# Loads, transposes and a batch's first stage moved within the prologue of an FFT and FFN kernel

## The chip, the cores and the metric

The kernel runs on one core of a Trainium2 chip. Its time is the device time of that core in microseconds (us), the median of several executions. A core has five engines that each work through their own list of instructions in order: PE (TensorE, matrix products), DVE (VectorE), ACT (ScalarE), POOL (GpSimd) and SP (SyncE). DMA transfers are issued from the lists of SP, ACT and POOL, and an issue that must wait for something holds up everything behind it in its list.

## What is computed

```python
def _attn_ref(x, filt_r, filt_i):
    X = np.fft.rfft(x, axis=1)
    F = (filt_r + 1j * filt_i)[None, :, :]
    Y = X * F
    y = np.fft.irfft(Y, n=x.shape[1], axis=1)
    return y.astype(np.float32)

def _moe_ref(x, w_in, w_out):
    h = np.maximum(x @ w_in, 0.0)
    return (h * h @ w_out).astype(np.float32)
```

x has 8 batches of 3008 rows and 256 columns in float32. Each batch goes through a real FFT along its rows, is multiplied by a filter (1505 frequencies by 256 columns, a real and an imaginary part), and comes back through the inverse FFT. The 24064 rows then go through a feed-forward network: w_in (256 x 2048), the square of the positive part, w_out (2048 x 256).

## The kernel before

**The FFT of a batch** is done as matrix products with constant tables, since 3008 = 64 x 47. It has four stages. *Stage A* (`unit_a`, 16 units for each batch from 1 on): one product over the 47, PSUM tile psA, copied to the tile u by ACT (even units) or DVE (odd units, batches 1 and 2); four units fill one tile u, which SP writes to a buffer dU in device memory (`write_u`). `read_u` brings it back in another order as ut. *Stage B* (`unit_b`, 12 units): products of ut with the table sSB (psB); DVE multiplies by the filter sF into prod, and for batches from 1 on two DMAs on POOL add the two halves of prod. *Stage P* (`unit_p`): products with the table sSP (psP), copied to ze, written to dZ; `read_z` brings dZ back as zt, in four parts c. *Stage Y* (`unit_y`, 16 units): products of zt (psY), copied to yt, the input of the network.

**Batch 0 is done ahead of everything else**, in a prologue, by other means. x is loaded in six halves (`load_wide` on SP, 512 KB each, in the order of `HALVES`), cast by DVE (`cast_wide`), and `chunk_a0` does stage A so that its output uT lies transposed; four passes, two classes of rows each. `turn_u` turns uT back with eight products with a unit matrix (psT), six calls in all, each copied to ut by two engines that it is given. Then a loop over k does two `unit_b` (whose output is first copied by ACT into ub), one `turn_u` and one `unit_p0`. Banks of PSUM come in turn from three tags (psH, psF, psO, two buffers each) through `bank_pair`. `turn_f` (DVE) puts the second half of the filter in place, once for each quarter of it (`FC`).

**Loads on POOL** go in this order before the change: a one-element copy into `tiny` that waits for the second half-load of x and so holds the rest back; 18 loads of the filter in four quarters; both halves of w_in (`load_win`, two loads each); the first two of eight loads of batch 1's x (`load_x`). When the products of the prologue are issued, `load_rest` follows: a second copy into `tiny`, which waits for zt, then the other x loads and w_out (`load_wout`). SP carries the loads of x, the tables (`load_const`), dZ, zt, dU, ut and all stores of the result.

**The trip of z.** Between the last `unit_p0` and the first `unit_y` dZ is written and read back. PE does 22 products of zeros there (`fill`, 128 x 512), which nothing uses.

**The main loop** has 8 turns s for each of 47 groups of 512 rows. Turn s does `ffn_g1` (psH: four products of 512 columns, with ACT's positive part into h), part of the second product of the group before (`ffn_g2` for the first and last group, `products` with `sums` for the rest, a scheme with seven products in place of eight), and DVE's square (`ffn_sq`). w_in's first half is read in turns 0 to 3 of a group, its second half in turns 4 to 7; w_out from turn 8 on. The FFT work of batches 1 to 7, and the end of batch 0's, is laid between by `fft_plan`: each unit has a due time in turns; `fixed` units have their half-turn, `units` look for a free one near theirs, and `moves` (loads, reads, `settle_f`, `settle_sp`) are added to theirs. For batch 1 the list has all 16 `unit_a` at turns 3 to 11.5, `read_u` at 12.5, `unit_b` from 16.5 to 30, and the first `unit_y` at 38. By the rule of `fft_plan` the last `unit_p` of batch 1 falls on turn 34, after the change on 33.5; the last `unit_a` of batch 2 on 44.5, after the change on 42. `settle_f` and `settle_sp` bring the filter and sSP from the form that batch 0 uses to that of the others.

Of the kernel before, what the change touches and what calls it, by code (L numbers as in the profile page):

```python
# [104 lines left out]
def kernel(  # L105
# [9 lines left out]
    nc = tc.nc  # L115
# [64 lines left out]
    def load_x(b, k):  # L180

        c, i = divmod(k, 2)
        if i == 0:
            x16s[(b, c)] = p_x16.tile([96, 8, D], F16, tag="x16", name=f"x16_{b}_{c}")
        t = x16s[(b, c)][:, 4 * i:4 * i + 4, :]
        m = slice(8 * c + 4 * i, 8 * c + 4 * i + 4)
        if b + 1 < B:
            v = xrows[b * S:b * S + 96 * NM, :].rearrange("(p m) d -> p m d", m=NM)
            nc.gpsimd.dma_start(out=t, in_=v[:, m, :])
        else:  # L190
            v = xrows[b * S:b * S + S, :].rearrange("(p m) d -> p m d", m=NM)
            nc.gpsimd.dma_start(out=t[0:80], in_=v[0:80, m, :])
            nc.gpsimd.dma_start(out=t[80:94], in_=v[80:94, m, :])
# [11 lines left out]
    xw16, xw32 = {}, {}  # L205
# [60 lines left out]
    def load_win(i):  # L266
        c = slice(1024 * i, 1024 * i + 1024)
        for k in range(2):
            nc.gpsimd.dma_start(out=sWin[:, k, c], in_=moe_w_in[128 * k:128 * k + 128, c])

    def load_wout(i):
        c = slice(8 * i, 8 * i + 8)
        nc.gpsimd.dma_start(out=sWout[:, c, :],
                            in_=moe_w_out.rearrange("(jt r) c -> r jt c", r=128)[:, c, :])
# [7 lines left out]
    for k in range(2):  # L282
        c = slice(12 * k, 12 * k + 12)
# [1 line left out]
        load_const(sSP[:, c, :], dPA, k)  # L285
        load_const(sSPx[k], dPB, k)
    tiny = const.tile([1, 2], F16, name="tiny")
    nc.gpsimd.tensor_copy(out=tiny[:, 0:1], in_=xw32[1][0:1, 0, 0:1])
    for c in FC:
        load_f(*c)  # L290
    for k in range(2):
        load_win(k)
    for k in range(2):
        load_x(1, k)

    def load_rest():

        nc.gpsimd.tensor_copy(out=tiny[:, 1:2], in_=ztiles[0][0:1, 0, 0:1])
        for k in range(2, 6):
            load_x(1, k)  # L300
        for k in range(2):
            load_wout(k)
        for k in range(6, 8):
            load_x(1, k)

    def fill(n):

        ps = psO("fill").rearrange("p a d -> p (a d)")
        for _ in range(n):
            nc.tensor.matmul(ps, zero[:, 0:128], zero, start=True, stop=True)  # L310
# [25 lines left out]
    def chunk_a0(k, *cs):  # L336

        for c in cs:
            banks, groups = bank_pair(f"psA_0_{c}_{k}")
            for dt in range(2):  # L340
                for i in range(4):
                    m = 4 * k + i
                    o = banks[dt][:, 96 * i:96 * i + 96]
                    d = slice(128 * dt, 128 * dt + 128)
                    nc.tensor.matmul(o, xw16[2 * (c % 2)][:, m, d], s0[:, c // 2, :],
                                     start=True, stop=False)
                    nc.tensor.matmul(o, xw16[1][0:120, m, d], s0[0:120, 2 + c, :],
                                     start=False, stop=True)
            for dt in range(2):
                m = 32 * c + 16 * k  # L350
                o = uT[:, dt, :, m:m + 16].rearrange("p c (m q) -> p m c q", q=4)
                pv = banks[dt][:, 0:384].rearrange("p (m c q) -> p m c q", m=4, q=4)
                if (pair_engine() is nc.scalar) if len(groups) == 1 else (dt == 0):
                    nc.scalar.copy(out=o, in_=pv)
                else:
                    nc.vector.tensor_copy(out=o, in_=pv)

    def turn_u(k, *engs):

        banks, groups = bank_pair(f"psT_{k}")  # L360
        for i in range(4):
            for dt in range(2):
                o = banks[i // 2][:, (i % 2) * D + 128 * dt:(i % 2) * D + 128 * dt + 128]
                nc.tensor.matmul(o, uT[:, dt, 4 * k + i, :], ident, start=True, stop=True)
        for i in range(2):
            eng = engs[i % len(engs)]
            o = uts[0][:, 4 * k + 2 * i:4 * k + 2 * i + 2, :]
            pv = banks[i].rearrange("p (a d) -> p a d", d=D)
            if eng is nc.scalar:
                eng.copy(out=o, in_=pv)  # L370
            else:
                eng.tensor_copy(out=o, in_=pv)
# [271 lines left out]
    def fft_plan():  # L644

        fixed, units, moves = [], [], []
        for b in range(1, B):
            f = (b * S // TG) * SLOTS - (48 if b > 1 else 40)
            d = 0
            if b == 1:  # L650
                for n in range(4, 16):
                    fixed.append(((n if n < 8 else n + 2 if n < 12 else 2 * n - 7) + n % 2 / 2,
                                  unit_y, 0, n))
                moves.append((7.5, read_z, 0, 3))
                for a in range(16):
                    fixed.append(((3 if a < 8 else 4) + a / 2, unit_a, b, a))
                for q in range(8):
                    moves.append((1 + q, settle_f, 3 * q, 3 * q + 3))
                moves.append((4, settle_sp))
                moves.append((12.5, read_u, b))  # L660
                d = 7
            else:
                for a in range(16):
                    if a % 2 == 0 and b > 2:
                        moves.append((f + ((-57 + 2.3 * a) if b == 3 else (-66 + 2.75 * a)),
                                      load_x, b, a // 2))
                    units.append((f + (-16 + a, -46 + 2.1 * a, -56 + 2.75 * a)[min(b, 4) - 2],
                                  unit_a, b, a))
                moves.append((f + (5.5 if b == 2 else -6.5), read_u, b))
            for p in range(12):  # L670
                r = 16.5 + 13.5 * p / 11 if b == 1 else 9 + 25 * p / 11 if b == 2 else -2 + 36 * p / 11
                units.append((f + r, unit_b, b, p))
                if b == 1 and 2 <= p < 10:
                    moves.append((f + r, load_x, 2, p - 2))
                units.append((f + r + (4 if b == 1 else 7 - 2.5 * p / 11), unit_p, b, p))
            for c in range(4):
                moves.append((f + (40 + d / 14 * 3, 43, 48, 54)[c] - d, read_z, b, c))
            for n in range(16):
                (fixed if n < 4 else units).append((f + YN[n] - d, unit_y, b, n))
        work, used, done = {}, set(), {}  # L680
        for r, *u in fixed:
            h = int(2 * r)
            used.add(h)
            work.setdefault(h, []).append(u)
        rank = (unit_b, unit_p, unit_y, unit_a)
        for r, *u in sorted(units, key=lambda u: (rank.index(u[1]), u[0])):
            after = done.get((u[0], u[1]), -1)
            h = min((h for h in range(max(int(2 * r) - 3, after + 1), int(2 * r) + 12)
                     if h not in used),
                    key=lambda h: (sum(h + i in used for i in (-2, -1, 1, 2)) > 2) * 2  # L690
                    + abs(h - int(2 * r)))
            used.add(h)
            done[(u[0], u[1])] = h
            work.setdefault(h, []).append(u)
        for r, *u in moves:
            work.setdefault(int(2 * r), []).append(u)
        return work
# [7 lines left out]
    for n, cs in enumerate(((0, 2), (0, 2), (1, 3), (1, 3))):  # L705
        for h in HALVES[n + 2:n + 3] if n > 1 else HALVES[2 * n:2 * n + 2]:
            cast_wide(*h)
        chunk_a0(n % 2, *cs)
    uts[0] = p_ut.tile([128, NC, D], F16, tag="ut", name="ut_0")
    turn_u(0, nc.scalar, nc.vector)  # L710
    turn_u(1, nc.scalar, nc.scalar)
    turn_u(2, nc.scalar, nc.vector)
    for k in range(8):
        if k < 6:
            for p in (2 * k, 2 * k + 1):
                for c in FC:
                    if c[0] == 2 * p:
                        turn_f(*c)
                if k > 1 and p % 2:
                    unit_p0(k - 2)  # L720
                unit_b(0, p)
        if 0 < k < 4:
            turn_u(k + 2, nc.scalar, nc.vector)
        if k > 5:
            unit_p0(k - 2)
    read_z(0, 0)
    read_z(0, 1)
    load_rest()
    fill(22)
    for n in range(4):  # L730
        unit_y(0, n)
    prologue[0] = False
# [5 lines left out]
    for s in range((NG + 1) * SLOTS):  # L738
        g, k = divmod(s, SLOTS)
# [46 lines left out]
```

## Time and profile before

| what | value |
|---|---|
| median of 7 runs | 775.01 us (772.49 to 779.17) |
| the profiled execution, its time | 774.29 us |
| its span from first to last instruction | 772.2 us |
| PE busy | 744.5 us (96%) |
| DVE busy | 646.9 us (84%) |
| ACT busy | 571.9 us (74%) |
| POOL busy | 188.5 us (24%) |
| mean granted clock of TensorE | 0.989 |
| first psH of the main loop | 51.14 us |

In the profile's lists a line gives its start and its length in us, the engine, the line of the kernel, the operation, the tile written and the tiles read, and how many instructions were merged; in brackets stands the idle time of the engine ahead of it and what ended that. "POOL ... DMA_DIRECT2D" is the issue of a transfer, not the transfer. The busy time of PE is modelled from the pipelined products, so a product's length includes its drain.

### The profile page before, as it was taken

What the parts mean: (1) busy time and instruction counts of PE and PEld (TensorE: products, weight loads), DVE (VectorE), ACT (ScalarE), POOL (GpSimd) and SP (SyncE); (2) the same over time, 40 slices, a digit from 0 to 9 for tenths busy, and PEclk for the clock granted to TensorE, in tenths of its full rate; (3) what the DMA queues carried; (4) which work ended last, traced back from release to release, by engine and by line L of the source; (5) the groups of instructions that cost most, each with busy time, mean ns of one, the idle gap of its engine ahead of it and who ended that gap; (6) DMA issues with size and microseconds to landing.
All of it is one profiled execution on the core that took longest, in us unless ns stands there. A gap on an engine that the chain in (4) does not pass through costs nothing.

```text
span 772.2 us, 19474 instructions
## 1 busy us (share of the span) xinstructions
PE 744.5 (96%) x8148; PEld 547.2 (71%) x8148; DVE 646.9 (84%) x734; ACT 571.9 (74%) x843; POOL 188.5 (24%) x262
## 2 busy tenths in 40 slices
PE   6777999999999999999999999999999999999998
PEld 3644666777778777777778777787777777777776
DVE  4748898799979898898889889798989999878873
ACT  2646777778877887778877887778887777777773
POOL 4320382033403232223212323133311232000000
PEclk8799999999999999999999999999999999999999
DMA  9987699477677546764677455855447433321011
GB/s 301 184 179 151 153 178 224 123 186 145 130 199 150 114 103 150 211 135 90 121 188 171 104 127 110 205 135 123 99 97 214 97 76 96 97 70 55 29 57 56
DMA packets 107184, 104.87 MB, mean 136 GB/s; under 512 B 9960, under 2 KB 94504, under 8 KB 106200
## 3 DMA queue, kind: packets, MB, share of 16 engines
q1 hardware_dynamic: 82408, 77.80, 33.6%
q0 software_dynamic: 24544, 25.64, 24.2%
q8 instruction: 64, 1.05, 0.5%
q10 hardware_dynamic: 144, 0.18, 0.1%
q14 instruction: 24, 0.20, 0.1%
HBM read 58.95 MB, written 48.23 MB: 139 GB/s over the span
## 4 chain that ended last, share of the span: by engine, by line
PE 84%; DVE 8%; DMA 3%; issue 2%; ACT 2%; SPq 1%; POOL 0%; ACTq 0%; DVEq 0%
PE psH L505 37%; PE psX L618 19%; PE psY L618 14%; PE psY L475 3%; PE psA L326 2%; PE psB L387 2%; PE psP L439 2%; DVE h L516 2%; DVE prod L400 2%; PE psO L525 2%; DMA prod<-prod 1%; DMA dZ<-ze 1%; DMA zt<-dZ 1%; PE fill L310 1%; DVE sum L591 1%
## 5 line engine op out<-in xcount | busy, mean ns | idle before, releaser
L509 ACT ACTIVATE h<-psH 128x1024 f16<-128x1024 f32 x376 | 384.9, 1024 | 154.8 <-PE psH L505 152.7
L505 PE MATMUL psH<-yt,sWin 128*128 128x512 f16 (+7 forms) x1728 | 387.5, 352 | 1.4 <-DVE yt L484 1.0
L516 DVE TENSOR_TENSOR h<-h 128x2048 f16<-128x2048 f16 (+1 forms) x192 | 229.8, 1197 | 47.4 <-ACT h L509 47.1
L407 POOL DMA_DIRECT2D prod<-prod x168 | 139.7, 970 | 432.5 <-DVE prod L400 390.1
L505 PEld LDWEIGHTS <-sWin 128*128 128x128 f16 x1728 | 152.3, 98 | 101.5 <-issue 6.1
L618 PEld LDWEIGHTS <-sum 128*128 128x128 f16 x2880 | 177.6, 98 | 20.0
L618 PEld LDWEIGHTS <-h 128*128 128x128 f16 x2160 | 133.7, 98 | 20.9
L400 DVE TENSOR_TENSOR prod<-psB,sF 128x1024 f16<-128x1024 f32 x84 | 102.3, 1219 | 13.6 <-PE psB L387 13.5
L618 PE MATMUL psX<-sT,sum 128*128 128x128 f16 x1440 | 102.4, 219 | 0.0
L618 PE MATMUL psY<-sT,sum 128*128 128x128 f16 x720 | 69.6, 219 | 0.0
L330 ACT CAST u<-psA 96x512 f16<-96x512 f32 x96 | 55.6, 580 | 2.7 <-PE psA L326 2.3
L594 DVE TENSOR_TENSOR sum<-sum,h 128x2048 f16<-128x2048 f16 x45 | 55.0, 1222 | 1.0
L618 PE MATMUL psY<-sWout,h 128*128 128x128 f16 x720 | 55.0, 219 | 0.0
L618 PE MATMUL psX<-sT,h 128*128 128x128 f16 x720 | 54.9, 219 | 0.0
L618 PE MATMUL psY<-sWout,sum 128*128 128x128 f16 x720 | 54.7, 219 | 0.0
L597 DVE TENSOR_TENSOR sum<-h 128x2048 f16<-128x2048 f16 x45 | 54.8, 1217 | 0.0
L600 DVE TENSOR_TENSOR sum<-h,sum 128x2048 f16<-128x2048 f16 x45 | 54.7, 1216 | 0.0
L591 DVE TENSOR_TENSOR sum<-h 128x2048 f16<-128x2048 f16 x45 | 54.7, 1216 | 0.0
L484 DVE CAST yt<-psY 128x376 f16<-128x376 f32 x62 | 33.7, 544 | 24.8 <-PE psY L475 24.8
L475 PEld LDWEIGHTS <-zt 112*128 112x128 f16 x512 | 34.1, 99 | 22.2 <-issue 8.4
L441 ACT CAST ze<-psP 128x512 f16<-128x512 f32 x84 | 49.0, 583 | 0.4 <-PE psP L439 0.2
L475 PE MATMUL psY<-sC,zt 112*128 112x94 f16 x512 | 43.2, 207 | 6.0 <-DMA zt<-dZ 3.6
(70 smaller groups left out, 612.9 us busy)
## 6 DMA issues: line engine op xcount, KB each, us to landing
zt<-dZ SPq DMA_DIRECT2D x64, 192.0 KB
dU<-u SPq DMA_DIRECT2D x28, 384.0 KB
prod<-prod POOLq DMA_DIRECT2D x168, 64.0 KB, 2.8
dZ<-ze SPq DMA_DIRECT2D x28, 384.0 KB
x<-in_x_dram POOLq DMA_DIRECT2D x48, 192.0 KB, 5.2
ut<-dU SPq DMA_DIRECT2D x7, 1024.0 KB
out_dram<-top SPq DMA_DIRECT2D x31, 128.0 KB
out_dram<-bot SPq DMA_DIRECT2D x31, 128.0 KB
```

The lines of the kernel that those rows point to most:

```text
L330: nc.scalar.copy(out=o, in_=pv)
L400: nc.vector.tensor_mul(out=prod, in0=pv.unsqueeze(1).to_broadcast([128, 2, 2, D]), in1=sF[:, :, 2 * p:2 * p + 2, :])
L407: nc.gpsimd.dma_start(out=prod[64 * i:64 * i + 64, 0], in_=prod[64 - 64 * i:128 - 64 * i, 1], accum_op=mybir.AluOpType.add)
L475: nc.tensor.matmul(ps[:, 94 * jj:94 * jj + 94], zt[:, 4 * (g % 2) + jj, dt * 128:(dt + 1) * 128], sSY, start=True, stop=True)
L505: nc.tensor.matmul(ps[:, i, o:o + n], sWin[:, dt, jt * 128:(jt + 1) * 128], yts[b][:, dt, r:r + n], start=(dt == 0), stop=(dt == 1))
L509: nc.scalar.activation(out=h2[:, 2 * s:2 * s + 2, :], in_=ps, func=AF.Relu)
L516: nc.vector.tensor_mul(out=v, in0=v, in1=v)
L591: nc.vector.tensor_add(out=t, in0=a21, in1=a22)
L594: nc.vector.tensor_sub(out=t, in0=f[5], in1=a11)
L597: nc.vector.tensor_sub(out=t, in0=a11, in1=a21)
L600: nc.vector.tensor_sub(out=t, in0=a12, in1=f[6])
L618: nc.tensor.matmul(o[:, t, :], f[p][:, q, 128 * t:128 * t + 128], sg["w"][p][:, q, :], start=(m == 0 and p in (1, 2)), stop=(q == 7), skip ...
```

## The change

The first copy into `tiny` reads the fourth half-load of x instead of the second, so the loads of the filter wait for that. Behind the filter, POOL loads x of batch 1 (parts 0 and 1, then 2 to 5, which stand after `chunk_a0` in the program) and only then the first half of w_in. The second half of w_in, x parts 6 and 7 and w_out follow behind the second copy into `tiny`. Four and two products of zeros are added after the first two passes of `chunk_a0`. Two `turn_u` instead of three are done ahead of the loop, and the third one in its first trip; the second one is copied by ACT and DVE instead of ACT alone. In the trip of z twelve `unit_a` of batch 1 take the place of 16 of the 22 fills. `fft_plan` keeps the four others at turns 8 to 9.5 and has new due times for batches 1 and 2.

```diff
-    nc.gpsimd.tensor_copy(out=tiny[:, 0:1], in_=xw32[1][0:1, 0, 0:1])
+    nc.gpsimd.tensor_copy(out=tiny[:, 0:1], in_=xw32[1][0:1, 4, 0:1])
     for c in FC:
         load_f(*c)
     for k in range(2):
-        load_win(k)
-    for k in range(2):
         load_x(1, k)
 
     def load_rest():
 
         nc.gpsimd.tensor_copy(out=tiny[:, 1:2], in_=ztiles[0][0:1, 0, 0:1])
-        for k in range(2, 6):
+        load_win(1)
+        for k in range(6, 8):
             load_x(1, k)
         for k in range(2):
             load_wout(k)
-        for k in range(6, 8):
-            load_x(1, k)
...
                 moves.append((7.5, read_z, 0, 3))
-                for a in range(16):
-                    fixed.append(((3 if a < 8 else 4) + a / 2, unit_a, b, a))
                 for q in range(8):
                     moves.append((1 + q, settle_f, 3 * q, 3 * q + 3))
-                moves.append((4, settle_sp))
-                moves.append((12.5, read_u, b))
+                moves.append((10, settle_sp))
+                for a in range(12, 16):
+                    fixed.append((2 + a / 2, unit_a, b, a))
+                moves.append((10.5, read_u, b))
...
-                moves.append((f + (5.5 if b == 2 else -6.5), read_u, b))
+                moves.append((f + (2 if b == 2 else -6.5), read_u, b))
             for p in range(12):
-                r = 16.5 + 13.5 * p / 11 if b == 1 else 9 + 25 * p / 11 if b == 2 else -2 + 36 * p / 11
+                r = 14 + 15 * p / 11 if b == 1 else 6 + 28 * p / 11 if b == 2 else -2 + 36 * p / 11
                 units.append((f + r, unit_b, b, p))
                 if b == 1 and 2 <= p < 10:
                     moves.append((f + r, load_x, 2, p - 2))
-                units.append((f + r + (4 if b == 1 else 7 - 2.5 * p / 11), unit_p, b, p))
+                units.append((f + r + (4.5 if b == 1 else 7 - 2.5 * p / 11), unit_p, b, p))
             for c in range(4):
-                moves.append((f + (40 + d / 14 * 3, 43, 48, 54)[c] - d, read_z, b, c))
+                moves.append((f + (40 + d / 14, 43, 48, 54)[c] - d, read_z, b, c))
...
         chunk_a0(n % 2, *cs)
+        if n < 2:
+            fill(4 - 2 * n)
     uts[0] = p_ut.tile([128, NC, D], F16, tag="ut", name="ut_0")
+    for k in range(2, 6):
+        load_x(1, k)
+    load_win(0)
     turn_u(0, nc.scalar, nc.vector)
-    turn_u(1, nc.scalar, nc.scalar)
-    turn_u(2, nc.scalar, nc.vector)
+    turn_u(1, nc.scalar, nc.vector)
...
-        if 0 < k < 4:
+        if k < 4:
             turn_u(k + 2, nc.scalar, nc.vector)
...
     load_rest()
-    fill(22)
+    for a in range(12):
+        unit_a(1, a)
+    fill(6)
     for n in range(4):
         unit_y(0, n)
```

## The prediction

> **What bounds the kernel now.** I read the slices of the page first, then the busy times of four stretches (columns: start:end, length, then busy time and count of PE, weight loads, DVE, ACT, POOL, then granted clock, DMA share, GB/s).
>
> ```profile
> PE   6777999999999999999999999999999999999998
> PEclk8799999999999999999999999999999999999999
> ...
> 0.00:51.10 51.10, 36.26 (x308) 25.86 (x309) 27.13 (x46) 21.29 (x37) 18.20 (x36) 0.85 0.90 223
> 51.10:84.90 33.80, 29.11 (x183) 16.55 (x182) 25.10 (x41) 22.36 (x30) 1.38 (x3) 0.98 0.80 168
> 84.90:140.00 55.10, 51.28 (x545) 36.59 (x544) 50.67 (x55) 40.82 (x63) 26.34 (x36) 1.00 0.85 182
> 140.00:772.20 632.20, 627.84 (x7119) 468.18 (x7116) 544.03 (x594) 487.44 (x714) 142.57 (x188) 1.00 0.52 123
> ```
>
> From 140 us on PE idles 4.4 us of 632: nothing to gain there, and whatever the start gives reaches the end whole. What can move is the prologue up to the first psH at 51.14 us, the turns s = 0 to 15 (PE idle 33.80 - 29.11 = 4.7 us) and batch 1 (55.10 - 51.28 = 3.8 us idle). Next the clock in single microseconds, and the order of time of DVE, PE and POOL in the prologue.
>
> ```profile
> 14.00:15.00 1.00, 0.00 (x0) 0.00 (x0) 1.00 (x2) 0.00 (x0) 0.07 (x1) 0.91 1.11 314
> 15.00:16.00 1.00, 0.95 (x13) 0.95 (x14) 0.00 (x0) 0.00 (x0) 0.00 (x0) 0.50 1.09 306
> ...
> 25.00:26.00 1.00, 0.37 (x6) 0.20 (x3) 0.77 (x2) 1.00 (x3) 1.00 (x3) 0.97 0.95 138
> ...
> 49.00:50.00 1.00, 0.95 (x12) 0.98 (x13) 0.00 (x0) 0.44 (x1) 1.00 (x3) 0.50 0.90 141
> ```
>
> ```profile
> 25.41 0.69 DVE L372 CAST ut<-psT 128x512 f16<-128x512 f32 x1 [0.23 <-PE psT L364]
> 26.13 1.25 DVE L248 COPY sF<-sF 64x1536 f16<-64x1536 f16 x2
> ...
> 26.25 1.03 PE L387 MATMUL psB<-ut,sSB 128*128 128x256 f16 x8 [0.88 <-DVE ut L372]
> 41.78 4.91 PE L310 MATMUL fill<-zero 128*128 128x512 f16 x22
> 49.05 0.47 PE L475 MATMUL psY<-sC,zt 112*128 112x94 f16 x4 [2.25 <-DMA zt<-dZ]
> ...
> 7.07 0.70 POOL L288 CAST tiny<-xw 1x1 f16<-1x1 f32 x1 [6.63 <-DMA xw<-in_x_dram]
> 22.91 0.57 POOL L241 DMA_DIRECT2D sF<-in_filt_r_dram  x1 [2.31 <-DMA sF<-in_filt_r_dram]
> 24.22 0.57 POOL L241 DMA_DIRECT2D sF<-in_filt_i_dram  x1
> 24.78 2.17 POOL L269 DMA_DIRECT2D sWin<-in_moe_w_in_dram  x4
> 47.10 0.18 POOL L298 COPY tiny<-zt 1x1 f16<-1x1 f16 x1 [19.09 <-DMA zt<-dZ]
> ```
>
> The clock is at 0.50 from 14.8 to 25.9 us, and again from 49.0 to 52.3. The first product (psB) waits for the copy of the third turn_u, not of the first. PE is through with unit_p0 at 41.78, fills, and waits for zt until 49.05.
>
> **1. The gate on POOL.** The four `load_const` issues on SP at 7.03, 8.49, 9.78 and 11.06 wait for halves 2 to 5 of x, so the fourth landed near 9.8. The gate moves by some 2.6 us, and 18 filter issues, the x loads and win(0) behind it move with it. Does anyone wait? A POOL issue here waits for the one eight before it (the tensors named fit). So FC0 had landed by 19, FC1 by 24.2 (the issue at 24.22 no longer waits), and FC3, last issued at 24.2, by 32 with the median 7.4 us of the filter loads. DVE turned them at 26.13, 29.41 and 38.15: slack of 5 to 7 us. Take off 2.6 here and some 3.6 for an earlier DVE (below) and between +1 and -1 us is left: hidden, but barely; if not, up to 2 us. Halves 5 and 6 were not waited for (the casts at 14.32 and 18.77 follow the DVE operation ahead of them at once): no gain there.
>
> **2. Fills of 4 and 2.** At 0.216 us (four psH take 0.86), 0.9 and 0.4 us, in PE gaps of 1.7 us (9.9 to 11.6) and 1.25 us (13.8 to 15.05) that wait for casts: free. They matter if they hold the clock. The two passes of chunk_a0 that ran at 0.50 took 2.65 us each (15.05 to 17.7, 19.5 to 22.2); at full clock 1.3 less each.
>
> **3. turn_u.** Before, psB starts 26.25 - 22.18 = 4.1 us after the first psT. With two turns ahead and banks psF free, it needs 16 transposes (2.47 us for 23 at half clock, so 0.107 each, 0.054 at full) beside one copy of 0.69: about 1.5 us. DVE copies turn 1 before turn_f, so its loop starts at 21.8 instead of 26.13: 4.3 earlier. The loop is DVE's (9.06 us busy in 30 to 40 us), and turn 2's half adds 0.69 there. Prologue: **-3.5 us**. At half clock the loop starts at 24.8, which with the 0.69 leaves -0.6; the other end is -4.3.
>
> **4. Twelve unit_a for 16 fills, in the trip of z.** PE 12 x 0.22, DVE 6 x 0.69, ACT 6 x 0.57, both idle there for 6.8 and 7.0 us. Two psF banks alternate, ACT on one, DVE on the other; DVE's rounds of 0.38 (matmul with drain) + 0.69 = 1.07 us bind. Six rounds from the end of the ze copy (43.29) end PE's part at 49.0 on the old scale, and fill(6) adds 1.3 at full clock: psY is 1.25 us late against zt; at half clock 2.5. Against that, a warm clock at 49 to 52 saves 1.05 us on four unit_y (0.52 apart now) and 0.85 on eight psH (2.57 us against 1.73). Sum **0** (-0.65 to +2.5). The three write_u stand on SP behind read_z(0,0) and (0,1) and ahead of read_z(0,2), which waits for psY anyway. Their x, issued by 31 us on POOL, lands 7.9 us later by the median, near 39: psA of a = 8 is due at 42.
>
> The trace shows no gap of PE longer than 2 us before the clock fell at 14.8; the window before it was some 40% busy. [...]
>
> **5. Turns 0 to 15 without those units.** PE is rid of 12 x 0.22 = **-2.6 us**. DVE is rid of 4.1 us where it is nearly full (9.07 of 10 us in 60 to 70), so part of the 4.7 us of idle PE goes: **-2.2** (0 to -4.1). What could be late: win(1) now stands behind the gate on zt (47.10, some 43.6 after). Two issues, done at 45; by the sWin rows (6.6 to 9.5 us) landed at 51 to 54; turn 4, which reads it, comes at 52.5. wout landed 61 to 65 (issues at 49.6 and 50.5, 11.7 and 14.7 us), at most 18.1 us behind the gate. By the KB of the issue rows the queues then moved 4 x 192 of x, 2 x 512 of wout, 384 of sSP and 384 of u; now 2 x 256 of sWin, 2 x 192 of x, 2 x 512 of wout and 3 x 384 of u, 3072 for 2560 KB: landed between 43.6 + 18.1 = 61.7 and a fifth later, 65.3, and due at 62 to 63 (turns 8, 9). For both I take **+0.5** (0 to +3).
>
> **6. Batch 1 and 2.** unit_b starts at s = 14 instead of 16.5, spread over 15 turns instead of 13.5; DVE is full at 90 to 110, PE idle there for 2.4 us: **-0.7** (0 to -2.4). read_u follows the last unit_a by one turn as before, the next unit_b 3.5 turns after it (4 before). The last unit_p falls on s = 33.5 instead of 34, psY stays at 38, so the wait below shrinks by half a turn, 1 us: **-0.9** (0 to -1.35).
>
> ```profile
> 133.72 0.33 PE L475 MATMUL psY<-sC,zt 112*128 112x94 f16 x4 [1.35 <-DMA zt<-dZ]
> ```
>
> Batch 2: read_u at 42 directly behind its last unit_a, first unit_b at 46: four turns, 8.2 us, against 8.5 us that this trip took in batch 1 (psA 76.4 to psB 84.89): **+0.4** (0 to 1.2). SP's stores wait behind it for some 3.6 us (77.5 to 81.14); three ost buffers cover that. settle_sp at s = 10 instead of 4: sSP is needed at 18.5, and the trips on SP are 4 us: nothing.
>
> **Sum.** -3.5 + 0 - 2.6 - 2.2 + 0.5 - 0.7 - 0.9 + 0.4 = -9.0 us. Span 772.2 becomes 763.2; the execution takes 2.1 us more (774.29), the median of the seven runs stands 0.7 above that: **766.0 us**. A difference under 0.5% (3.9 us) can't be told from none.
>
> **Rivals.**
> - *Filters late.* The slack of part 1 is spent, DVE waits up to 3.5 us in turn_f, 3 more than I allow. For it: 22.91 shows POOL waiting for filter data. Against: with x out of the way they are faster. 769. Chance 0.17.
> - *The fills don't hold the clock* (0.50 in 15 to 26 and 49 to 52 again): the prologue gives 0.6 and the trip costs 1: 766.0 + 2.9 + 1 = 770. For it: 40% busy was not enough. [...] 0.13.
> - *Weights behind the gate land late.* If win(1) needs the 14.7 us of wout's slowest load it lands at 59.5, 7 us after turn 4 is ready: 766.0 + 7 - 0.5 = 772.5, no change. Against: it is first in the queue, wout was behind four x loads. 0.13.
> - *Slower: the twelve units hold psY.* They stand ahead of it in PE's queue, and wait for x(1,2..5), which POOL now issues behind all filters. Each us beyond 42 costs one; all is lost from a landing at 51, and it is slower by 0.5% from 55, 24 us after the issue. Against: the slowest x landing in the trace is 15.1 us, so 46, which would cost 4. With a landing at 56: 766 + 14 = 780. 0.06.
> - The forecast: 0.51, own range 761 to 769.
>
> Good ends for the four terms that have them (-4.3, -0.65, -4.1, -2.4 for -3.5, 0, -2.2, -0.7) give 766.0 - 5.0 = 761, a little of batch 1's waits 760; at the other side the range takes in the rivals up to the late weights: 760 to 772.5, with the slow one left out. Faster 0.80, same 0.13, slower 0.07.
>
> **What would show it.** PEclk near 1.0 in 15 to 26; first psB near 21 and the last psP near 38; POOL's gate near 9.8; turn_f without waiting for sF; psY of batch 0 near 46.8, behind psA and fill, not zt; turn 16 near 76 us (84.0 before); the wait at 133.72 under 0.5. I am wrong if DVE waits for sF, psA for x, or psH for sWin by more than 1 us each, or if the idle PE time of 51 to 85 stays although the units are gone.

## The result, and the profile after

The changed kernel takes 770.19 us (median of 13 runs, 768.39 to 771.54), the kernel before 774.84 (median of 34 runs on the same chips): ratio 0.9937, 95% interval 0.9922 to 0.9953. It is faster by 4.65 us, more than the 0.5% that tells it from no change, and about half of the forecast gain. One of the 34 runs took 1989.56 us, and the ratio leaves it out. The profiled execution took 770.55 us with a span of 768.4; the one of before 774.29 and 772.2.

The page's slices of the changed kernel, then the busy times of the first three of the four stretches and of four shorter ones (columns as before):

```profile
PE   6778999999999999999999999999999999999998
PEclk9989999999999999999999999999999999999999
```

```profile
0.00:51.10 51.10, 35.90 (x299) 22.72 (x300) 30.93 (x52) 23.92 (x41) 18.85 (x38) 0.91 0.97 238
51.10:84.90 33.80, 29.86 (x202) 17.88 (x201) 25.20 (x39) 21.23 (x28) 2.75 (x4) 0.93 0.79 178
84.90:140.00 55.10, 53.08 (x573) 38.05 (x571) 50.91 (x57) 43.13 (x67) 23.68 (x33) 1.00 0.84 174
...
18.00:19.00 1.00, 0.61 (x8) 0.61 (x9) 0.33 (x1) 0.00 (x0) 0.53 (x1) 0.61 1.17 326
46.00:47.00 1.00, 0.70 (x2) 0.20 (x1) 0.69 (x1) 0.26 (x1) 1.00 (x3) 0.50 1.14 197
60.00:65.00 5.00, 1.90 (x14) 0.87 (x13) 4.76 (x12) 2.58 (x4) 0.00 (x0) 1.00 1.24 250
65.00:70.00 5.00, 4.88 (x20) 2.60 (x20) 2.60 (x5) 1.68 (x3) 0.00 (x0) 0.66 0.04 9
```

PE's idle time in the second stretch is 33.80 - 29.86 = 3.9 us, where it was 4.7: it stayed, although the units are gone. In the third it fell from 3.8 to 2.0. The clock is at half from about 18.2 to 21.6 us, again from 45.5 to 52.3, and it is down in 65 to 70. In 60 to 65 PE is busy for 1.90 of 5 us, and DVE for 4.76.

The order of time of the changed kernel shows where that is; first POOL's two gates (the copies into `tiny`) and turn_f, then PE in the trip of z:

```profile
9.96 0.18 POOL L288 CAST tiny<-xw 1x1 f16<-1x1 f32 x1 [9.52 <-DMA xw<-in_x_dram]
24.32 1.14 DVE L248 COPY sF<-sF 64x1536 f16<-64x1536 f16 x2
45.06 0.18 POOL L296 COPY tiny<-zt 1x1 f16<-1x1 f16 x1 [14.44 <-DMA zt<-dZ]
...
42.23 0.59 PE L323 MATMUL psA<-x,sC 94*96 94x512 f16 x2 [0.67 <-ACT u L327]
43.38 0.59 PE L323 MATMUL psA<-x,sC 94*96 94x512 f16 x2 [0.56 <-DVE u L329]
...
47.43 2.76 PE L307 MATMUL fill<-zero 128*128 128x512 f16 x6
50.21 0.52 PE L472 MATMUL psY<-sC,zt 112*128 112x94 f16 x4
```

The first z lands 2.04 us earlier than before (45.06 for 47.10), but psY starts 1.16 us later (50.21 for 49.05), 5.1 us behind its z. It stands in PE's queue behind the last of the twelve stage A products and the six fills, which take 2.76 us at half clock. Then the turns (those of DVE and PE about turn 8, and POOL's issue of w_out):

```profile
47.36 1.81 POOL L273 DMA_DIRECT2D sWout<-in_moe_w_out_dram  x2
...
61.76 1.22 DVE L513 TENSOR_TENSOR h<-h 128x2048 f16<-128x2048 f16 x1
62.99 0.36 DVE L253 TENSOR_SCALAR sF<-sF 64x768 f16<-64x768 f16 x1
63.38 0.35 DVE L255 COPY sF<-sF 64x768 f16<-64x768 f16 x1
63.74 0.36 DVE L253 TENSOR_SCALAR sF<-sF 64x768 f16<-64x768 f16 x1
64.14 0.35 DVE L255 COPY sF<-sF 64x768 f16<-64x768 f16 x1
64.52 0.55 DVE L481 CAST yt<-psY 128x376 f16<-128x376 f32 x1
62.05 0.38 PE L502 MATMUL psH<-yt,sWin 128*128 128x512 f16 x1
65.12 0.81 PE L502 MATMUL psH<-yt,sWin 128*128 128x512 f16 x3 [2.69 <-DVE yt L481]
68.09 1.69 PE L502 MATMUL psH<-yt,sWin 128*128 128x512 f16 x4
70.93 1.03 PE L502 MATMUL psH<-yt,sWin 128*128 128x512 f16 x4
...
130.39 0.33 PE L472 MATMUL psY<-sC,zt 112*128 112x94 f16 x4 [0.31 <-DMA zt<-dZ]
```

PE waits 2.69 us for the yt copy of unit_y(0,7), which stands in DVE's queue behind one square of h and two calls of settle_f (two rows each, 62.99 to 64.49). That is nearly all of the 2.9 us for which psH waits for such copies in the whole run. Behind it comes half clock: the four psH of turn 9, at 68.09, take 1.69 us, those of turn 10 again 1.03. From the ninth to the tenth h it is 3.85 us, where it was 2.18: by this estimate the clock costs 1.7 us on top of the wait. The last row is the wait of batch 1 for zt, 1.35 us before.

Points of the trace that tell the terms apart (start in us; "h" is ACT's copy of one psH, one in each turn, so the ninth belongs to turn 8):

```
                             before   after   gain so far
turn_f                        26.13   24.32     1.81
last psP of batch 0           41.67   39.76     1.91
gate on zt (POOL)             47.10   45.06     2.04
first psY                     49.05   50.21    -1.16
1st h (turn 0)                52.88   53.79    -0.91
9th h (turn 8)                67.74   65.97     1.77
10th h (turn 9)               69.92   69.82     0.10
17th h (turn 16)              84.92   83.53     1.39
73rd h (turn 72)             201.65  197.88     3.77
last h                       760.15  756.37     3.78
```

### The profile page after: what moved, and what is told of

It reads as the page before. It is cut to its first block, busy times and chain, and to the rows that moved or that the text cites. A ratio compares the mean times of both kernels' runs of the same rounds, so it can differ in the third digit from the quotient of the medians.

```text
span 768.4 us, 19455 instructions
## 1 busy us (share of the span) xinstructions
PE 742.8 (97%) x8138; PEld 544.2 (71%) x8138; DVE 647.0 (84%) x735; ACT 572.2 (74%) x842; POOL 187.9 (24%) x262
## 4 chain that ended last, share of the span: by engine, by line
PE 82%; DVE 8%; DMA 6%; POOL 1%; issue 1%; ACT 1%; SPq 0%; DVEq 0%; POOLq 0%; ACTq 0%
PE psH L502 37%; PE psX L615 19%; PE psY L615 14%; PE psY L472 3%; PE psA L323 3%; DVE h L513 2%; PE psB L384 2%; PE psP L436 2%; DVE prod L397 2%; PE psO L522 2%; DMA sF<-in_filt_i_dram 1%; DMA xw<-in_x_dram 1%; DVE sum L588 1%; DMA x<-in_x_dram 1%; DMA prod<-prod 1%
## 5 line engine op out<-in xcount | busy, mean ns | idle before, releaser
L615 PE MATMUL psX<-sWout,h 128*128 128x128 f16 x720 | 47.6, 219 | 0.0
```

Of the source, the lines that this page charges most:

```text
L615: nc.tensor.matmul(o[:, t, :], f[p][:, q, 128 * t:128 * t + 128], sg["w"][p][:, q, :], start=(m == 0 and p in (1, 2)), stop=(q == 7), skip ...
```

## The experiments

All are edits of the changed kernel and compute everything. Each result gives the median in us, the number of runs, and the ratio to the kernel before, run beside it on the same chip, with its interval. Results of different sets are compared by these ratios: the kernel before had medians of 774.8 to 776.4 us in them.

**e1, the fills of 4 and 2 taken out.**

```diff
-        if n < 2:
-            fill(4 - 2 * n)
```

> The changed kernel without the fills of 4 and 2 behind the first two passes of chunk_a0. Theory A (the fills keep the granted clock up for one more window, no longer): the clock falls at 14.8 us again as before the change, the third pass takes 2.65 us instead of 1.4, turn_f starts near 25.5 us instead of 24.3, and the time is 1.0 to 1.3 us over the changed kernel's, 771.3. Theory B (the fills do nothing, the earlier start comes from the two turn_u alone): turn_f within 0.3 us of 24.3, time as the changed kernel's, 770.2.

771.52 us (10), 0.9957 [0.9943, 0.9971]. The clock fell at 12.5 us and stayed at half for 10.2 us (in the changed kernel from 18.21 for 3.4), turn_f came at 25.25 and the last psP at 41.38, 1.6 us later than with the fills. That is Theory A (the falls of before and of the change lie 3.39 us apart). Nine more profiles below have the same two fills (turn_f at 22.51 to 24.65 us): in none is the clock at half for longer than 3.4 us ahead of 37 us, while it was for 10.2 us in both kernels without them (before, from 14.8, and e1). The fills are worth about 1.3 us by the medians; the intervals overlap, so the size is loose.

**e2, the gate on POOL back at the second half-load.**

```diff
-    nc.gpsimd.tensor_copy(out=tiny[:, 0:1], in_=xw32[1][0:1, 4, 0:1])
+    nc.gpsimd.tensor_copy(out=tiny[:, 0:1], in_=xw32[1][0:1, 0, 0:1])
```

> The changed kernel with the filter loads let go behind the second half-load of x, as before the change. Theory A (nobody waits for the filter or for the halves of x): turn_f and every psP within 0.3 us of the changed kernel's, time 770.2 within 1. Theory B (the later gate leaves the transfers to x, so that the casts come earlier): casts of halves 5 and 6 at least 1 us later, turn_f at 25.3 or later, time 771 to 772. Theory C (the filter held the changed kernel up without showing it): turn_f or the products earlier, time 769 or less.

770.24 us (6), 0.994 [0.9921, 0.9959]. The gate opens at 6.91 us instead of 9.96. In its profile turn_f comes 0.3 us later (24.65) and the last psP 1.0 later, most of it after the clock fell at 39.2; the median is the changed kernel's. By that the move of the gate is worth nothing in either direction.

**e3, the changed prologue alone:** the trip of z with 22 fills, and the stage A units and due times of batches 1 and 2 as before (settle_sp stays at turn 10).

```diff
-    for a in range(12):
-        unit_a(1, a)
-    fill(6)
+    fill(22)
...
-                for a in range(12, 16):
-                    fixed.append((2 + a / 2, unit_a, b, a))
-                moves.append((10.5, read_u, b))
+                for a in range(16):
+                    fixed.append(((3 if a < 8 else 4) + a / 2, unit_a, b, a))
+                moves.append((12.5, read_u, b))
...
```

> The changed kernel with the trip of z and the plan of turns as before the change (22 fills, 16 units in turns 3 to 11.5, due times of batches 1 and 2 as before): the prologue's part alone. Theory A (the prologue gives 1.9 us, the twelve units cost 3 us in the trip and give it back later): first psH with data near 49.8 us, 1.9 ahead of before, and the rest as before: 772.9. Theory B (the twelve units in the trip are the whole gain): 774.8, as before the change. Theory C (the twelve units are a net loss): 770 or less.

774.37 us (12 runs, 771.97 to 779.53), 1.0004 [0.9982, 1.0027]: no gain that can be measured, nearer to Theory B. In its profile the prologue does what the forecast said, and the clock with it (here against the changed kernel's own row of the same stretch):

```profile
18.40:22.00 3.60, 2.60 (x40) 2.02 (x37) 1.93 (x4) 2.26 (x5) 1.95 (x5) 1.00 1.20 214
```

```profile
18.40:22.00 3.60, 3.17 (x37) 2.84 (x38) 1.12 (x2) 0.96 (x2) 1.73 (x4) 0.55 1.21 217
```

The first row is e3: full clock, turn_f at 22.51, last psP at 37.94, 3.7 us ahead of before. The first h is 2.6 ahead, turns 72 to 136 still 1.8; then a psY of a later batch, at 321.53, waits 1.4 us for its zt, 1.55 us are gone, and at the last h it is 0.25 behind. So in this execution the prologue's gain did not reach the end, and the loss came where z of a later batch was late.

**e4, the second half of settle_f later** (turns 9 to 12 instead of 5 to 8), away from the yt copy that PE waits for.

```diff
-                    moves.append((1 + q, settle_f, 3 * q, 3 * q + 3))
+                    moves.append((1 + q if q < 4 else 5 + q, settle_f, 3 * q, 3 * q + 3))
```

> The changed kernel with the last four settle_f at turns 9 to 12 instead of 5 to 8. Theory A (PE's wait of 2.7 us at 62 us is for DVE's queue, in which the copy of unit_y(0,7) stands behind squares and settle_f): the ninth h comes near 63 us instead of 65.97, the clock stays at 1.0 from 65 to 70, the time is 3 to 4.5 us under the changed kernel's, 766 to 767. Theory B (the weights behind the gate land late, w_out between 61 and 65 us, and DVE only happens to be busy): PE waits as long, now for w_out, and the time is within 1 us of 770.2.

769.82 us (6), 0.9931 [0.9909, 0.9952]: no better than the change. Two rows from its order of time, and its clock:

```profile
62.55 0.81 PE L502 MATMUL psH<-yt,sWin 128*128 128x512 f16 x3 [0.65 <-DVE yt L481]
...
68.05 1.03 PE L522 MATMUL psO<-sWout,h 128*128 128x256 f16 x8 [2.30 <-DMA sWout<-in_moe_w_out_dram]
```

```profile
65.00:70.00 5.00, 2.70 (x15) 1.44 (x14) 1.65 (x4) 1.49 (x2) 0.00 (x0) 0.91 0.34 83
70.00:75.00 5.00, 5.00 (x33) 3.22 (x32) 4.25 (x9) 2.61 (x4) 0.00 (x0) 0.75 0.60 164
```

The wait for DVE shrank from 2.69 to 0.65 us and the ninth h came at 63.40 instead of 65.97. Five microseconds later PE waits 2.30 us for w_out, whose loads took 14.7 and 19.8 us, and the clock falls afterwards. In the changed kernel's profile the same loads took 13.5 and 16.8 us, and nobody waited for them. The 17th h, 83.41, is where it was (83.53). Neither theory in full: the wait that was named is real, and a second one takes its place.

**e5, e4 and w_out loaded ahead of the gate on zt.**

```diff
 (e4, and)
+        for k in range(2):
+            load_wout(k)
         nc.gpsimd.tensor_copy(out=tiny[:, 1:2], in_=ztiles[0][0:1, 0, 0:1])
...
-        for k in range(2):
-            load_wout(k)
```

> As the kernel with the last four settle_f later, and w_out issued ahead of the second copy into tiny, right behind win(0), instead of at the end of load_rest. Theory A (with DVE's queue out of the way w_out's landing at 68 us is the bound of turn 9, 2.3 us of waiting and a clock that falls in it): no wait for sWout, the tenth h near 65.6 us at most 68 (71.2 for the eleventh before), the time 3 us under that kernel's 769.8, 766 to 767.5. Theory B (1 MB more ahead of the trip of z slows dZ and zt, or x): the second copy into tiny later than 46.5 us instead of 45.06, and a time of 769 or more.

771.19 us (6), 0.9942 [0.9921, 0.9963].

```profile
50.40 0.18 POOL L298 COPY tiny<-zt 1x1 f16<-1x1 f16 x1 [17.46 <-DMA zt<-dZ]
...
53.57 0.47 PE L472 MATMUL psY<-sC,zt 112*128 112x94 f16 x4 [3.46 <-DMA zt<-dZ]
```

With the weights under way at the same time z lands 5.3 us later, and psY waits 3.46 us for it. From the first to the 17th h it then takes 57.74 to 84.26 = 26.5 us, 3.2 less than in the change. Theory B for the time: with settle_f and w_out out of the way the turns are faster, and loading w_out in the trip costs as much as it saves.

**e6, fill(6) taken out** (the diff is that line).

> The changed kernel without the six fills between the last unit_a and unit_y. Theory A (the trip's overrun is paid, but turn 9 waits for DVE and w_out anyway): first h 2.5 us earlier than in the changed kernel, near 51.2, the tenth h (69.82) at most 1 us earlier, the time 769.2 to 770.2. Theory B (the overrun of the trip goes through to the end): the time 767.5.

770.6 us (6), 0.9932 [0.9912, 0.9952]. Its clock held in the prologue, so turn_f came at 22.52, psY at 48.07 and the first h at 52.23, 1.6 us earlier than in the change; PE then waits 2.69 us for the same yt copy (at 64.37), and the tenth h is 0.8 us ahead, the 17th 0.75, the 73rd 0.1. The time is near Theory A's, but the trip itself was not shortened: the clock was at half from 37.2 to 54.3 us, and from the last psP to the first h it took 13.8 us (14.0 in the change). The early first h is the prologue's, so this run does not show what the trip without fills is worth.

**e7, e5 with unit_y 0 to 3 laid between stage A units 8 to 11, and no fill** (the line of fill(6) is out too).

```diff
-    for a in range(12):
+    for a in range(8):
         unit_a(1, a)
...
         unit_y(0, n)
+        unit_a(1, 8 + n)
```

> As the kernel with w_out early, and the first four unit_y laid between the last four of the twelve unit_a, without fill: psY is then due when zt has landed. Theory A (psY stood 5 us behind zt because of the twelve units ahead of it, and with the two later bounds gone this counts): first psY near 46 us, first h near 49.5 (53.8 in the changed kernel), the time 3 us under the kernel with w_out early, 763 to 764. Theory B (something later in turns 0 to 13 takes it back, as DVE's 25 us of work in that stretch): within 1 us of the kernel with w_out early.

772.89 us (12), 0.9974 [0.9959, 0.9989].

```profile
52.69 0.47 PE L472 MATMUL psY<-sC,zt 112*128 112x94 f16 x4 [7.73 <-DMA zt<-dZ]
```

It tells little of the order of psY: with w_out ahead of the trip z was late again, and PE waited 7.73 us for it in front of four units that it could have done. Inconclusive; the same order without e5's move was not tried.

**e8, a third fill, of 6, behind the third pass.**

```diff
-        if n < 2:
-            fill(4 - 2 * n)
+        if n < 3:
+            fill((4, 2, 6)[n])
```

> The changed kernel with six more fills behind the third pass of chunk_a0. [...] Theory B (the clock falls there whatever is filled in): turn_f within 0.4 us of 24.3 and the time 770.2.

769.95 us (6), 0.9927 [0.9905, 0.9949]. Three rows: one stretch in e4, the same stretch in e8, and a later one in e8:

```profile
14.45:17.86 3.41, 1.61 (x32) 1.46 (x32) 1.71 (x4) 0.86 (x2) 1.02 (x2) 1.00 1.11 319
14.45:17.86 3.41, 2.95 (x39) 1.94 (x38) 1.70 (x4) 0.86 (x2) 0.57 (x2) 1.00 1.11 319
...
18.00:19.00 1.00, 0.63 (x14) 0.64 (x15) 0.31 (x1) 0.07 (x1) 1.00 (x3) 1.00 1.15 332
```

The clock stays at 1.00 from 12 to 41 us, turn_f comes at 23.17 and the last psP at 38.60. Without the third fill the clock held in the prologue of some profiles too (e3, e6), so this alone shows little. But e4's clock fell at 17.86, with PE busy for 1.61 of the 3.41 us ahead; e8's did not, with 2.95. (e8's fell at 41.73, which is 23.87 us or seven times 3.41 later.) So in this profile Theory B fails for the clock and for turn_f (23.17 for 24.3), and holds for the time (769.95 for 770.2). The first h is at 51.69, 2.1 us ahead of the change; the 17th, at 82.70, only 0.8: PE waits the same 2.69 us for yt, and the clock is then at half from 62.2 to 69.0.

**e9, e4 and two of the three writes of u of batch 1 moved from the trip to turns 8 and 8.5.** So 768 KB fewer are to be written ahead of turn 8, while w_out is under way.

```diff
 (e4, and)
-        if i == 3:
+        if i == 3 and not (b == 1 and c in (1, 2)):
...
+                moves += [(8, write_u, b, 1), (8.5, write_u, b, 2)]
```

> As the kernel with the last four settle_f later, and two of the three writes of u that were moved into the trip (768 of 1152 KB) put back to turns 8 and 8.5. Theory A (the DMA engines are full from the gate on zt to w_out's landing, so what is moved ahead of it delays it): w_out lands at 65 us or earlier instead of 68, no wait for sWout, the tenth h near 65.6 and the eleventh near 67.7 us (71.2 before), the clock at 1.0 from 65 to 72, the time 767 instead of 769.8. Theory B (the writes of u do not touch w_out): it lands at 67 to 68 us, PE waits 2 us for it, the time within 0.7 us of 769.8.

766.31 us (6), 0.987 [0.9842, 0.9898]: better than the change, the intervals don't touch. (The kernel before had 776.44 us in this set; by the times alone it is 3.9 us below the change.)

```profile
65.00:70.00 5.00, 5.00 (x38) 3.37 (x37) 4.16 (x8) 3.15 (x5) 0.00 (x0) 1.00 0.68 179
70.00:75.00 5.00, 5.00 (x45) 3.50 (x43) 4.88 (x10) 3.64 (x5) 0.00 (x0) 1.00 0.84 250
```

PE is busy for all of both stretches, where e4 had 2.70 us in the first, and the clock holds. w_out landed in 12.3 and 14.0 us instead of e4's 14.7 and 19.8, and nobody waits for it. Counted from the gate on zt, its second half landed after 17.2 us (17.8 in e10), against 20.0 to 23.3 in the seven kernels that write u in the trip and load w_out behind the gate (the change, e1, e2, e4, e6, e8, e11). The 17th h comes at 79.37, 4.2 us ahead of the change, with the first where it was (53.68).

**e10, e9 without fill(6) and with e8's third fill.**

> As the kernel with u written later, without the six fills ahead of unit_y and with six more behind the third pass of chunk_a0. Theory A (the trip's overrun, not w_out, is now next): first h 2 to 2.7 us earlier, near 51.2, and the time 1.5 to 2.5 us under the kernel with u written later, 765. Theory B (w_out's landing, which follows the gate on zt, still sets turn 9): PE waits for sWout again and the time is within 1 us of that kernel's.

765.0 us (6), 0.9855 [0.9827, 0.9883], as Theory A said. First h 50.99, 17th 77.35, turn 72 10.0 us ahead of before, where e9 is 7.8 ahead. It is the fastest kernel of the study, but its interval overlaps with e9's.

**e11, the due times of batches 1 and 2 as before,** the twelve units staying in the trip (read_u at 12.5, unit_b from 16.5 over 13.5 turns, unit_p 4 turns later, and batch 2 in the same way).

> The changed kernel with the due times of batches 1 and 2 as before the change (read_u at 12.5, unit_b from 16.5 to 30, read_z at 34.5; batch 2's read_u and unit_b too); the twelve unit_a stay in the trip. Theory A (the earlier dues are worth what the changed kernel gains on the one before between turns 16 and 72, 2.4 us): 772.6, psY of batch 1 waiting for zt 1.3 us again. Theory B (they are worth the 1.2 us of the forecast): 771.4. Theory C (nothing): 770.2.

773.73 us (12 runs, 770.85 to 776.46), 0.9959 [0.9939, 0.998].

```profile
131.57 0.33 PE L472 MATMUL psY<-sC,zt 112*128 112x94 f16 x4 [1.98 <-DMA zt<-dZ]
```

The wait that the change had brought to 0.31 us is back, at 1.98. Between the 17th and the 73rd h this kernel gives back 2.1 us (2.78 ahead of before, then 0.68), where the change gains 2.4. A later batch waits another 1.0 us for zt in its profile. The time lies beyond Theory A's 772.6; its interval overlaps with the change's, so the size is loose: 1.7 us by the ratios, 4.5 in this stretch of the two profiles.

**e12, e9's move of the writes alone,** settle_f as in the change.

> The changed kernel with the two writes of u at turns 8 and 8.5, and settle_f where the change left it. Theory A (two bounds stand one behind the other at turns 8 and 9: DVE's queue and w_out's landing; either alone gives next to nothing, both together the 3.9 us measured): PE waits some 2.7 us for the copy of yt again, the clock falls there, the tenth h is within 1 us of the changed kernel's 69.8 counted from the first h, the time 769 to 770.5. Theory B (the writes of u were the whole of it): no such wait and a time of 767 or less.

770.39 us (6), 0.9947 [0.9927, 0.9967].

```profile
63.42 0.87 PE L502 MATMUL psH<-yt,sWin 128*128 128x512 f16 x3 [2.69 <-DVE yt L481]
```

```profile
65.00:70.00 5.00, 5.00 (x26) 2.92 (x25) 1.54 (x3) 2.32 (x4) 0.00 (x0) 0.76 0.36 104
```

The wait for DVE is as long as in the change, to the hundredth, and the clock falls behind it. From the first to the tenth h it takes 68.11 - 52.09 = 16.0 us, as in the change (69.82 - 53.79): Theory A. Here w_out's second half landed 20.8 us behind the gate, so the move of the writes did not bring it earlier in every execution (they were issued at 61.9 us, with w_out still under way). The four kernels together:

```
ratio to before           u written in the trip        u written at turns 8, 8.5
settle_f at turns 5-8     0.9937 [0.9922, 0.9953]      0.9947 [0.9927, 0.9967]
settle_f at turns 9-12    0.9931 [0.9909, 0.9952]      0.9870 [0.9842, 0.9898]
```

Either edit alone is worth nothing that these runs can measure; both give 0.7%.

## Why the prediction was half right

The sign held, and 770.19 us lies in the range, which was wide (760 to 772.5); the forecast of 766.0 was 4.2 us too low. One of its own signs of being wrong came up: the idle PE time of 51 to 85 us stayed (3.9 for 4.7 us). The accounts, by the points of the trace (forecast, then measured):

```
part 1-3  prologue, to the last psP         -3.5    -1.9
part 4    trip of z, last psP to first h     0      +2.8
part 5    turns 0 to 15, 1st to 17th h      -4.3*   -2.3
part 6    17th to 73rd h                    -1.2    -2.4
          after that                         0       0.0
sum                                         -9.0    -3.8
* 2.6 + 2.2 less idle, + 0.5 for late loads
```

**Part 1, the gate, was right.** It opened at 9.96 us (9.8 said), turn_f never waited for sF, and by e2 its place is worth nothing that can be measured. The rival "filters late" falls with it.

**Part 2, the fills, was right with a limit.** They cost nothing and do hold the clock (without them, in e1, it is at half for 10.2 us, in the changed kernel for 3.4), but in the changed kernel's profile only 3.39 us longer: it fell at 18.21 instead of 14.82, and only one of the two slow passes became fast. The reading behind it had two slips: the clock before was at half until 25.06 and not 25.9 (0.97 in the row of 25 to 26), and again from 28.47 to 31.88, which the text does not mention. Where it says "some 40% busy", PE was busy, drains included, for 1.78 of the 3.41 us ahead of the fall at 14.82, 52%.

**Part 3 was mis-sized: -1.9 for -3.5.** The condition was named (-0.6 at half clock, -3.5 at full), and the profiled execution lies between. Seven profiles have the same code up to the last psP (the change, e3, e4, e6, e9, e11, e12): there the term measured 1.9 to 3.7 us, 3.3 to 3.7 in the three in which the clock held (e3, e6, e12). The mechanism, two turns ahead of the products, is as said; what failed is the step that took six fills to be enough for the whole of 15 to 26 us in every execution. That the profiled one lies at the low end of the seven is chance.

**Part 4 failed: +2.8 for 0.** The rounds were put at 1.07 us and came at 1.15 to 1.36, and the six fills at 1.3 and took 2.76, because the clock was at half from 45.5 to 52.3. The text itself put the bad end, at half clock, at +2.5, and then booked the warm clock's 1.9 us in the likely case; PE was busy for 1.78 of the 3.41 us ahead of the fall at 45.52. psY did wait "behind psA and fill, not zt", but 5 us behind its z, not 1.25. How much of it reached the end is not settled. In the profiles of e6 and e8 the first h came 1.6 and 2.1 us earlier than in the change and the 73rd 0.1 and 0.7; in e12's, 1.7 us earlier, and the 73rd 2.0. No run has the trip alone at full clock.

**Part 5 is where the rest went: -2.3 for -4.3.** "DVE is rid of 4.1 us where it is nearly full, so part of the idle goes" counted DVE's load and not the order in its queue. At turn 8 the yt copy stood behind a square and two settle_f that were not moved, and PE waited 2.69 us. Between the two h PE's idle time fell by 1.0 us, not 2.2, and its busy time by 1.3, not 2.6, since the products behind the wait ran at half clock (rows of before and after, from the first h to the 17th):

```profile
52.88:84.92 32.04, 27.40 (x178) 16.02 (x177) 23.67 (x38) 22.36 (x30) 0.00 (x0) 1.00 0.78 167
53.79:83.53 29.74, 26.07 (x170) 15.44 (x169) 22.02 (x34) 19.32 (x24) 1.38 (x2) 0.94 0.76 178
```

"Late loads, +0.5" named the right loads (3072 KB for 2560) at somewhat too low a price: w_out was to land 18.1 to 21.7 us behind the gate, and its second half landed after 20.0 in the change's profile and after 20.5 to 23.3 in the six others with the same loads behind the gate. With PE's wait for DVE lifted (e4) that cost 2.30 us; in the change it did not show, since PE came to it only at 69.84. The two bounds lie one behind the other, and the table of four kernels shows that only lifting both lets the time through; on top of the wait came a fall of the clock (a mean of 0.66 in 65 to 70 us in the change, 0.75 in 70 to 75 in e4). With both lifted the stretch took 79.37 - 53.68 = 25.7 us for the change's 29.7, more than the forecast's own gain.

**Part 6 was too small: -1.2 for -2.4.** Direction and place are as said (the wait 1.35 to 0.31), and e11 supports the cause: the same stages with the old due times lose 2.1 us there. From the 73rd h on the change keeps its gain whole, as forecast; e3 and e11 did not keep theirs.

**The rivals.** "The fills don't hold the clock", at 770, has the measured time, and half of its mechanism: the clock did fall in both of its places. But it can't be called the cause: with the clock held through the prologue in e8's profile the time was the same within the intervals. "Weights behind the gate land late" named the right resource, the wrong weights (w_out, not win(1)), and a wait that was covered by another, as e4 showed. "The twelve units hold psY" happened in kind, for psY was behind them, but by their own rounds and the fills; x was not late.

**Still open.** Why before (8.3 us over 33 runs), e3 (7.6), e11 (5.6) and also e4, e9 and e10 (4.9 to 5.3) spread more than the changed kernel (3.2) is not settled. Waits of 1.0 and 1.4 us for zt of later batches in the profiles of e11 and e3 fit it, e4's profile has none, and no run tested it. Nor is it settled why w_out's landing differs by 3 us between profiles with the same loads.

## What to carry to other kernels

Taking work out of a stretch pays only up to the next bound at its end: look for what stands ahead of the awaited instruction in its own queue, and for what the moved work sends ahead of a load that is due there. Where two waits lie one behind the other, as here, each edit alone can measure as nothing, so test them together before giving either up. Give the planner's due times the same shift as the work: without it, part of the gain was lost to a later wait for z.

## What the runs showed of the hardware

The granted clock changed in whole steps of 3.41 us. In e1, from half-microsecond windows:

```profile
12.50:13.00 0.50, 0.50 (x11) 0.50 (x9) 0.50 (x1) 0.17 (x2) 0.50 (x2) 0.53 1.07 430
22.50:23.00 0.50, 0.30 (x5) 0.31 (x6) 0.14 (x1) 0.00 (x0) 0.50 (x2) 0.73 0.25 32
39.50:40.00 0.50, 0.49 (x5) 0.20 (x4) 0.50 (x2) 0.06 (x1) 0.00 (x0) 0.83 1.12 328
53.00:53.50 0.50, 0.50 (x10) 0.50 (x8) 0.00 (x0) 0.14 (x1) 0.00 (x0) 0.52 1.04 159
```

A mean of 0.53 between 1.00 and 0.50 puts the first fall at 12.53; the rise follows at 22.77, the next fall at 39.83 and the rise at 53.48. The differences, 10.24, 17.06 and 13.65 us, are 3, 5 and 4 times 3.41. In the kernel before the falls at 14.82, 28.47 and 48.95 and the rises at 25.06, 31.88 and 52.36 lie 10.24, 3.41, 3.41, 17.07 and 3.41 us apart: 3, 1, 1, 5 and 1 times 3.41. Seven profiles with the same code up to turn_f had it at 22.51 us (e3) to 24.32 (the change); the clock's changes do not lie in the same places in them (falls at 17.86 us in e4, at 18.21 in the change), and the clock fell ahead of turn_f in four. So one profile can't settle a term of 2 us in a prologue. Before and after happen to have falls 3.39 us apart (14.82 and 18.21), nearly one step, which makes these two comparable.

A long gap of PE did not decide here: before the change the clock fell at 14.82 with no gap of PE longer than 1.72 us from its first product on. What went with the fall was the busy time of PE in the 3.41 us ahead of it: 1.78 us in the kernel before, 1.61 in the change (ahead of 18.21) and in e4 (ahead of 17.86), against 2.95 in e8, where the clock held. That is what four stretches of these profiles show, not a rule.
